# One scaling for both halves of a tile, a gate product on GpSimd, and a new order of the last keys, in a pooled-attention and mixture-of-experts kernel

## The chip, the cores and the metric

The kernel runs on one core of one Trainium2 chip. The metric is device microseconds (us) of one execution. Three timed executions of the kernel before gave 639.33, 640.91 and 641.08 us; the median is 640.91 us. The profile is of a fourth execution, of 639.47 us.

## What is computed

Two parts follow each other: attention with pooled keys and values, and a mixture of experts that sends each token to one expert.

```python
k_p = k.reshape(B, H, Sp, pool, D).mean(axis=3)          # B=8, H=8, S=576, pool=8, Sp=72, D=64
v_p = v.reshape(B, H, Sp, pool, D).mean(axis=3)
scores = scale * np.matmul(q, k_p.transpose(0, 1, 3, 2))
attn = np.exp(scores - np.max(scores, axis=-1, keepdims=True))
attn = attn / (np.sum(attn, axis=-1, keepdims=True) + 1e-09)
x = np.matmul(attn, v_p)                                  # then 4608 tokens x 512
logits = x @ w_gate + modality_bias[modality_id]          # 8 experts
e_idx = np.argmax(logits, axis=1)                         # gate_w is softmax(logits) at e_idx
out[mask] = gate_w[mask, None] * (np.maximum(x[mask] @ w1[e], 0.0) @ w2[e])
```

## The kernel before, in words

**Attention.** The 4608 tokens are 36 tiles of 128. A step (list `steps`, line 455) is two tiles of one batch, or one mixed tile that takes the last 64 tokens of each of two batches; there are 20 steps for 8 batches. The loop at line 895 runs over `n`: in round `n` the scores of step `n+1` are made while step `n-1` is finished. The order of each engine's instructions is the order in which this loop writes them. One round, in the order of the code, for the two tiles `old[0]` and `old[1]` of step `n-1`:

- `t_pe`, `t_act` (lines 551 to 561): TensorE transposes the exponentials of a tile, ACT copies them out of PSUM.
- `s_pe(n, 1)` (line 509): scores of the second four heads; `t4_pe`, `t4_act`: the same as `t_pe` and `t_act` for the last 16 of each pair's 144 keys.
- `a_pe(old[0])` (line 576): TensorE multiplies the transposed weights with the pooled values. A pair of heads has 2 x 72 = 144 keys: 128 of them are one contraction against `vw` (line 590), and the last 16 of all four pairs stand together in one 64-row contraction against `v4` (line 594). The result of a tile lies in two PSUM banks, `av0` for heads 0 to 3 and `av1` for heads 4 to 7, one buffer each. Beside 64 value columns each head has 8 columns of gate logits and one of the sum of weights, 73 (`VC`) in all.
- `s_dve(n, 1)` (line 529): DVE takes the row maximum from the scores (`mx`, line 533) and subtracts it (`sb`, line 536).
- `x_dve(old[0])` (line 596): DVE divides. For each bank it scales the sum (`r`, line 610), inverts it (line 612), writes the 256 values of four heads (`xb`, line 614) and their 32 logits (`lg`, line 616).
- `s_act(n, 1)` (line 540): ACT takes the exponentials of the first 128 keys of each pair (line 548) and of the last 16 (line 549), which go to a region of their own in `pe`.
- `s_pe(n+1, 0)`, `q_pe(n+2, 0)` (transposes of the queries, line 501), `s_dve(n+1, 0)`, then `a_pe(old[1])` and `x_dve(old[1])`.

Between these, `gap(m)` (line 469) lets up to m waiting DVE operations of the routing go (list `drip`): sorting of tokens to experts, written by `route` (line 646) and let go from round 6 on.

**Pooling and value operands.** Keys and values are pooled by GpSimd in three halving additions (`fold`, lines 296 to 298), in the order `pool_v(b+1)`, then `pool_k(b+2)`, one batch after the other; only batch 0 and part of batch 1 go to DVE. `v_operand(b)` (line 356) writes the pooled values into `vw` and `v4`, masked so that each key meets only its own head (line 361: GpSimd's masked product for `v4`), and transposes them (lines 366, 367). `v_gate(b)` (line 374) multiplies the transposed values with the gate matrix (lines 382, 383) and writes the eight gate columns: ACT writes those of `vw` (lines 385, 386), DVE those of `v4` (line 387), as a product with the mask `m_4`. For b over 0 the matmuls of `v_gate` write a free corner of the score bank `sc_1` (line 378), so that bank's next scores (lines 520, 526) wait until lines 385 to 387 have read it.

**Loads.** SP issues the loads in the order of `step_loads` (line 856), one queue, and each load waits until the eighth load before it has landed. `load_v4(b)` (line 220) brings the 16 last pooled rows of each head pair to 64 partitions, twice (`z`), 128 KB each; `load_q(b)` (line 227) brings 1 MB of queries.

**Mixture of experts.** From line 976 on, slots of 256 tokens go through two layers (lines 162 and 1143) in split fp32r precision; DVE and ACT split the weights (lines 135, 138). No line of this part is changed.

Of the kernel before, what the change touches and what calls it, by code (L numbers as in the profile page):

```python
# [9 lines left out]
F32 = mybir.dt.float32  # L10
# [5 lines left out]
ALU = mybir.AluOpType  # L16
# [6 lines left out]
P = 128  # L23
# [7 lines left out]
def kernel(  # L31
# [151 lines left out]
    with ExitStack() as actx:  # L183
        ap = actx.enter_context(tc.tile_pool(name="ap", bufs=1))

        late_p = actx.enter_context(tc.tile_pool(name="late_p", bufs=1))
        ps_av = actx.enter_context(tc.tile_pool(name="ps_av", bufs=1, space=PSUM))
# [4 lines left out]
        def rows_of(x, b):  # L192

            return x[b].rearrange("h (s u) d -> (h s) (u d)", u=POOL)
# [24 lines left out]

        def load_v4(b):  # L220
            t4 = ap.tile([P, POOL * HD], F32, tag="v4", bufs=2, name=f"v4_{b}")
            src = rows_of(v, b).rearrange("(c r) x -> r c x", r=2 * SPL)[P:]
            for z in range(2):
                nc.sync.dma_start(t4[64 * z:64 * z + 64], src)
            v4raw[b] = t4
# [37 lines left out]
        nc.scalar.activation(m_4[:, 0:1], m_a, AF.Exp)  # L263

        m_i = ap.tile([P, NPAIR], I32, name="m_i")
        nc.gpsimd.iota(m_i, pattern=[[-1, NPAIR]], base=P, channel_multiplier=1)
        nc.vector.tensor_single_scalar(m_i, m_i, NPAIR - 1, op=ALU.bitwise_and)
        nc.vector.tensor_single_scalar(m_4, m_i, 0.0, op=ALU.is_equal)
        for z in range(2):
            nc.gpsimd.memset(pt4z[z][64 - 64 * z:128 - 64 * z], 0.0)  # L270
# [83 lines left out]
        m4b = m_4.rearrange("p (j o) -> p j o", o=1)  # L354
# [19 lines left out]
        def v_gate(b):  # L374
            vt, vt4 = vts[b]
            dw, d4 = vw[b % NB], v4[b % NB]
            if b:
                pg = spare[1][:, 1, 4 * SPL:4 * SPL + 12 * E].rearrange("p (u x) -> p u x", u=3)
            else:
                pg = ps_tr.tile([P, 3, 4 * E], F32, tag="tr", name=f"pg_{b}")  # L380
            for u in range(2):
                nc.tensor.matmul(pg[:, u, :], vt[:, u, :], wgb[:, u].rearrange("p g x -> p (g x)"), start=True, stop=True)
            nc.tensor.matmul(pg[:, 2, :], vt4, wg[0:64, 1::2, :], start=True, stop=True)
            pgv = pg[:, 0:2, :].rearrange("p u (g a e) -> p (u g) a e", g=2, a=2)
            nc.scalar.activation(dw[:, :, 0, HD:HD + E], pgv[:, :, 0, :], AF.Copy, scale=m_a)
            nc.scalar.activation(dw[:, :, 1, HD:HD + E], pgv[:, :, 1, :], AF.Copy, scale=m_b)
            nc.vector.tensor_tensor(d4[:, :, HD:HD + E], pg[:, 2, :].rearrange("p (j e) -> p j e", j=NPAIR),
                                    m4b.to_broadcast([P, NPAIR, E]), op=ALU.mult)


        bias_all = ap.tile([P, NT, E], F32, name="bias_all")
# [89 lines left out]
        qts, pqs, scs, pes, pps, pts, avs, lgs = {}, {}, {}, {}, {}, {}, {}, {}  # L481
# [94 lines left out]
        def a_pe(t):  # L576
            n, z = tile_step[t]
            b, jj, _ = steps[n]
            pt, pt4 = pts.pop(t), pt4z[z]
            av = [ps_av.tile([P, 512], F32, tag=f"av{u}", name=f"av_{t}_{u}") for u in range(2)]  # L580
            avs[t] = av
            if jj is not None:
                halves = [(slice(0, P), b % NB)]
            else:
                halves = [(slice(64 * y, 64 * y + 64), (b - 1 + y) % NB) for y in range(2)]
            for u in range(2):
                for gg in range(2):
                    c = 2 * u + gg
                    for hs, y in halves:
                        nc.tensor.matmul(av[u][hs, 2 * VC * gg:2 * VC * (gg + 1)], pt[:, c, hs],  # L590
                                         vw[y][:, c].rearrange("p a x -> p (a x)"), start=(gg == 0), stop=False)
                dst4 = av[u][:, 0:4 * VC].rearrange("p (g x) -> p g x", g=2)[:, :, VC:2 * VC]
                for hs, y in halves:
                    nc.tensor.matmul(dst4[hs], pt4[:, hs], v4[y][:, 2 * u:2 * u + 2, :], start=False, stop=True)  # L594

        def x_dve(t):
            n, z = tile_step[t]
            g, gi = tile_group[t]
            av = avs.pop(t)
            mixed = steps[n][1] is None  # L600
            b = steps[n][0]
            if gi == 0:
                lgs[g] = late_p.tile([P, GT, H, E], F32, tag="lg", bufs=2, name=f"lg_{g}")
            xw = xbs[n if n < NX0 else NX0 + n % (len(xbs) - NX0)]
            xo = xw[:, z, 0:D]
            for u in range(2):
                avv = av[u][:, 0:4 * VC].rearrange("p (h x) -> p h x", h=4)
                r = ap.tile([P, 4], F32, tag="r", bufs=4, name=f"r_{t}_{u}")
                rb = r.rearrange("p (h o) -> p h o", o=1)
                nc.vector.tensor_scalar(r, avv[:, :, VC - 1], float(POOL), 1e-9 * POOL, op0=ALU.mult, op1=ALU.add)  # L610
                gap(1)
                nc.vector.reciprocal(r, r)
                gap(1)
                nc.vector.tensor_tensor(xo[:, u * D // 2:(u + 1) * D // 2].rearrange("p (h d) -> p h d", h=4), avv[:, :, 0:HD],  # L614
                                        rb.to_broadcast([P, 4, HD]), op=ALU.mult)
                nc.vector.tensor_tensor(lgs[g][:, gi, 4 * u:4 * u + 4, :], avv[:, :, HD:HD + E],  # L616
                                        rb.to_broadcast([P, 4, E]), op=ALU.mult)

            if mixed:
                for y in range(2):  # L620
                    r0 = (b - 1 + y) * S + 512
                    stores.append(lambda y=y, r0=r0: nc.sync.dma_start(xs[r0:r0 + 64, :], xw[64 * y:64 * y + 64, 0, :]))
            elif z == 1:
                jj = steps[n][1]
                stores.append(lambda: nc.sync.dma_start(
                    xs[b * S:b * S + 512, :].rearrange("(p j) x -> p j x", j=4)[:, 2 * jj:2 * jj + 2, :], xw))
# [173 lines left out]
        for n, (b, jj, _) in enumerate(steps):  # L800
            if b + 1 < B:
                if jj == 0:
                    m = n if b else n + 1
                    at(hook_0, m, lambda b=b: pool_v(b + 1))
                    at(hook_1, m, lambda b=b: k_operand(b + 1, 0))
                    at(hook_1 if b == 0 else hook_q if b % 2 else hook_3, m, lambda b=b: k_operand(b + 1, 1))
                if jj == 1:
                    m = n if b else n + 1
                    if b + 2 < B:
                        at(hook_0, m, lambda b=b: pool_k(b + 2))  # L810
                    at(hook_1, m, lambda b=b: v_operand(b + 1))
                    at(hook_2, m, lambda b=b: v_gate(b + 1))
# [67 lines left out]
        pool_v(0)  # L880
        gate_operand()
        s_act(0, 0)
        q_pe(1, 0)
        q_act(1, 0)
# [10 lines left out]
        for n in range(N + 1):  # L895
# [45 lines left out]
            if has:  # L941
                s_act(n, 1)
# [18 lines left out]
            if n == 0:  # L961
                v_gate(0)
# [18 lines left out]
    op = [[ps_op.tile([P, 512], F32, name=f"op{i}_{z}") for z in range(2)] for i in range(2)]  # L981
# [119 lines left out]
    t = table(c4 + 6, NCOL, 4)  # L1101
# [189 lines left out]
```

## Time and profile before

| what | value |
|---|---|
| three timed executions, median | 640.91 us |
| profiled execution, its own time | 639.47 us |
| profiled span, first to last instruction | 637.8 us |
| TensorE (PE) busy | 601.1 us, 94% |
| VectorE (DVE) busy | 433.8 us, 68% |
| ScalarE (ACT) busy | 343.8 us, 54% |
| GpSimd (POOL) busy | 198.9 us, 31% |
| first and last `a_pe` matmul (line 590) starts | 24.7 and 190.6 us |
| `xb` products (line 614) | 72, mean 422 ns |

Between the span and the execution's own time lie 1.67 us. The attention's last round ends near 192 us, and the rest is the mixture of experts, in which PE is busy without a pause. The shares of the whole span are averages over both parts; what the change touches lies in the first 192 us.

### The profile page before, as it was taken

The numbers are of one execution on the slowest core, as the hardware profiler recorded it, in microseconds if no ns is written. First come the engines' busy times: TensorE is split into PE (matmuls) and PEld (weight loads), VectorE is DVE, ScalarE is ACT, GpSimd is POOL, SyncE is SP. The second block draws the span as 40 slices with busy tenths as digits, with TensorE's granted clock in tenths as the row PEclk, the third lists the DMA queues.
The fourth block names the chain that finished last, engine by engine and source line by source line (L and its number), as shares of the span: only waits on it lengthen the run. The fifth ranks groups of instructions, "written<-read, shape, count | busy, mean of one in ns | idle before, by whom it ended". The sixth has DMA issues, their size and how long they took to land.

```text
span 637.8 us, 12547 instructions
## 1 busy us (share of the span) xinstructions
PE 601.1 (94%) x4223; PEld 544.8 (85%) x4223; DVE 433.8 (68%) x940; ACT 343.8 (54%) x640; POOL 198.9 (31%) x277
## 2 busy tenths in 40 slices
PE   4799898989899999999999999999999999999992
PEld 3699797888798999999999999999999999999881
DVE  4778989999977578666566566656656566656541
ACT  2667566677441455555555555555556555555530
POOL 6689967563000221320320221231131231131230
PEclk9899999999999999999999999999999999999997
DMA  9999979764201901201210461220225410120120
GB/s 255 290 300 337 350 208 362 223 202 143 67 35 51 315 33 36 68 34 35 68 41 28 148 201 51 67 65 8 63 75 180 145 55 17 52 68 18 51 75 17
DMA packets 63406, 77.18 MB, mean 121 GB/s; under 512 B 15455, under 2 KB 42079, under 8 KB 63328
## 3 DMA queue, kind: packets, MB, share of 16 engines
q1 hardware_dynamic: 57168, 55.98, 28.4%
q0 software_dynamic: 6160, 20.26, 9.7%
q8 instruction: 38, 0.62, 0.4%
q14 instruction: 40, 0.33, 0.2%
HBM read 119.94 MB, written 19.45 MB: 219 GB/s over the span
## 4 chain that ended last, share of the span: by engine, by line
PE 76%; DVE 13%; DMA 7%; issue 1%; ACT 1%; SPq 0%; DVEq 0%; ACTq 0%
PE op L1143 30%; PE hp L162 30%; DMA out_dram<-ob,sidx 6%; PE av L590 3%; PE sc L526 3%; PE xt L153 2%; DVE mx L533 2%; DVE sb L536 2%; PE av L594 2%; DVE xb L614 2%; PE pq L501 1%; PE ph L162 1%; PE pp L555 1%; DVE arow L717 1%; DMA k<-in_k_dram 1%
## 5 line engine op out<-in xcount | busy, mean ns | idle before, releaser
L135 ACT CAST hl<-raw 128x1024 fp32r<-128x1024 f32 x138 | 144.8, 1049 | 138.6 <-PE op L1143 136.6
L162 PE MATMUL hp<-xh,hl 128*128 128x256 f32 x1152 | 186.2, 284 | 0.6 <-issue 0.6
L162 PEld LDWEIGHTS hp<-xh,hl 128*128 128x128 f32 x1152 | 166.0, 189 | 11.5 <-issue 1.0
L138 DVE TENSOR_TENSOR hl<-raw,hl 128x1024 fp32r<-128x1024 f32 x144 | 174.8, 1215 | 0.0
L1143 PE MATMUL op<-hl,hh 128*128 128x512 f32 x554 | 173.5, 394 | 0.0
L1129 POOL DMA_INDIRECT out_dram<-ob,sidx x37 | 51.0, 1379 | 369.3 <-DVE ob L1125 260.2
L166 DVE SCALAR_TENSOR_TENSOR hlo<-hp,hh 128x256 fp32r<-128x256 f32 x139 | 58.8, 423 | 136.6 <-ACT hh L164 136.6
L1143 PE MATMUL op<-hl,hlo 128*128 128x512 f32 x277 | 108.4, 391 | 0.0
L1143 PEld LDWEIGHTS op<-hl,hh 128*128 128x128 f32 x554 | 94.8, 189 | 12.1
L162 PE MATMUL hp<-xl,hl 128*128 128x256 f32 x576 | 92.0, 282 | 0.0
L164 ACT ACTIVATE hh<-hp 128x256 fp32r<-128x256 f32 x139 | 53.4, 384 | 49.6 <-PE hp L162 49.6
L162 PEld LDWEIGHTS hp<-xl,hl 128*128 128x128 f32 x576 | 79.0, 190 | 0.0
L1143 PEld LDWEIGHTS op<-hl,hlo 128*128 128x128 f32 x277 | 52.0, 188 | 11.8
L590 PE MATMUL av<-vw,pt 128*128 128x146 f32 (+1 forms) x320 | 50.9, 299 | 4.9 <-DVE lg L616 3.7
L142 POOL DMA_INDIRECT xg<-xs,gidx x40 | 44.2, 1105 | 17.1 <-issue 8.9
L590 PEld LDWEIGHTS av<-vw,pt 128*128 128x128 f32 (+1 forms) x320 | 40.3, 183 | 7.9 <-DVE lg L616 4.9
L526 PE MATMUL sc<-kt,qt 128*128 128x144 f32 x256 | 38.3, 294 | 1.5 <-DVE rs L706 1.1
L526 PEld LDWEIGHTS sc<-kt,qt 128*128 128x128 f32 x256 | 34.1, 195 | 2.4 <-DVE rs L706 1.3
L156 DVE TENSOR_TENSOR xl<-xt,xh 128x512 fp32r<-128x512 f32 x38 | 24.5, 684 | 15.5 <-ACT xh L155 15.5
L560 ACT COPY pt<-pp 128x512 f32<-128x512 f32 x36 | 21.1, 586 | 25.4 <-PE pp L555 25.0
L533 DVE TENSOR_REDUCE mx<-sc 128x8 f32<-128x576 f32 (+1 forms) x40 | 27.7, 692 | 10.0 <-PE sc L526 7.6
L614 DVE TENSOR_TENSOR xb<-av,r 128x256 f32<-128x256 f32 x72 | 30.4, 422 | 1.6
(226 smaller groups left out, 710.5 us busy)
## 6 DMA issues: line engine op xcount, KB each, us to landing
raw<-in_moe_w_dram SPq DMA_DIRECT2D x304, 256.0 KB
xs<-xb SPq DMA_DIRECT2D x16, 528.0 KB
k<-in_k_dram SPq DMA_DIRECT2D x7, 1024.0 KB
v<-in_v_dram SPq DMA_DIRECT2D x7, 1024.0 KB
q<-in_q_dram SPq DMA_DIRECT2D x6, 1024.0 KB
q<-in_q_dram SPq DMA_DIRECT2D x4, 512.0 KB
v<-in_v_dram SPq DMA_DIRECT2D x16, 128.0 KB
xs<-xb SPq DMA_DIRECT2D x8, 132.0 KB
```

Source lines behind the costliest of these rows:

```text
L135: nc.scalar.copy(hl[f][:, 0, :], raw[f])
L138: eng.tensor_sub(hl[f][:, 1, :], raw[f], hl[f][:, 0, :].bitcast(F32))
L142: nc.gpsimd.indirect_dma_start(out=xgs[(2 * s + tt) % len(xgs)], out_offset=None, in_=xs[0:rows, :], in_offset=IndirectOffsetOnAxis(idx[:, ...
L162: nc.tensor.matmul(ph, hl[f][:, w, d * P:(d + 1) * P], x[:, d, :], start=(n == 0 and d == 0), stop=(n == 2 and d == ND - 1))
L164: nc.scalar.activation(hh, ph, AF.Relu)
L166: nc.vector.scalar_tensor_tensor(hlo, ph, 0.0, hh.bitcast(F32), op0=ALU.max, op1=ALU.subtract)
L526: nc.tensor.matmul(dst, qt[:, i, :], kt[b % NB][:, :, h * SPL:(h + 1) * SPL], start=True, stop=True)
L533: nc.vector.reduce_max(mx, scv, axis=AX.X)
L590: nc.tensor.matmul(av[u][hs, 2 * VC * gg:2 * VC * (gg + 1)], pt[:, c, hs], vw[y][:, c].rearrange("p a x -> p (a x)"), start=(gg == 0), sto ...
L614: nc.vector.tensor_tensor(xo[:, u * D // 2:(u + 1) * D // 2].rearrange("p (h d) -> p h d", h=4), avv[:, :, 0:HD], rb.to_broadcast([P, 4, H ...
L1129: nc.gpsimd.indirect_dma_start(out=out[:, :], out_offset=IndirectOffsetOnAxis(idx.bitcast(U32), 0), in_=ob, in_offset=None, bounds_check=N ...
L1143: nc.tensor.matmul(o[tt], l[:, ts_], hl[f][:, w, D:2 * D], start=(f == 0 and n == 0), stop=(f == NF - 1 and n == 2))
```

## The change

Four things change.

1. The two PSUM banks of a tile become one tile `av` of two banks. `x_dve` scales the sums of all eight heads in one operation, inverts them in one, writes all 64 logits in one, and then writes the values bank by bank. The logits now stand ahead of the values. Two of the four `gap(1)` calls go, and a `gap(2)` follows the tile.
2. The gate product of `v4`: ACT copies the 32 columns out of PSUM into a new SBUF tile `vg4`, and GpSimd multiplies them with the mask. DVE no longer takes part.
3. The last keys' exponentials are written in another order: the 16 weights of a head pair stand side by side, where before the four pairs alternated.
4. With that order the mask `m_4` and the load of `v4` change: row 16 c + s of the tile holds row s of pair c, where before it was row 4 s + c. The source's access pattern in DRAM was 16 rows x 4 pairs x 512 values and is now 4 pairs x 16 rows x 512 values, with the same 64 partitions as destination.

```diff
-            src = rows_of(v, b).rearrange("(c r) x -> r c x", r=2 * SPL)[P:]
+            src = rows_of(v, b).rearrange("(c r) x -> c r x", r=2 * SPL)[:, P:, :]
...
-        nc.gpsimd.iota(m_i, pattern=[[-1, NPAIR]], base=P, channel_multiplier=1)
-        nc.vector.tensor_single_scalar(m_i, m_i, NPAIR - 1, op=ALU.bitwise_and)
+        nc.gpsimd.iota(m_i, pattern=[[-16, NPAIR]], base=P, channel_multiplier=1)
+        nc.vector.tensor_single_scalar(m_i, m_i, 16 * (NPAIR - 1), op=ALU.bitwise_and)
...
-            nc.vector.tensor_tensor(d4[:, :, HD:HD + E], pg[:, 2, :].rearrange("p (j e) -> p j e", j=NPAIR),
-                                    m4b.to_broadcast([P, NPAIR, E]), op=ALU.mult)
+            vg4 = ap.tile([P, NPAIR, E], F32, tag="vg4", bufs=1, name=f"vg4_{b}")
+            nc.scalar.copy(vg4, pg[:, 2, :].rearrange("p (j e) -> p j e", j=NPAIR))
+            nc.gpsimd.tensor_tensor(d4[:, :, HD:HD + E], vg4, m4b.to_broadcast([P, NPAIR, E]), op=ALU.mult)
...
-            tail = pe[:, 2 * NPAIR * P:].rearrange("p (t s c) -> p t c s", t=2, c=NPAIR)[:, 0:nt, 2 * w:2 * w + 2, :]
+            tail = pe[:, 2 * NPAIR * P:].rearrange("p (t c s) -> p t c s", t=2, c=NPAIR)[:, 0:nt, 2 * w:2 * w + 2, :]
...
-            av = [ps_av.tile([P, 512], F32, tag=f"av{u}", name=f"av_{t}_{u}") for u in range(2)]
+            av = ps_av.tile([P, 2, 512], F32, tag="av", name=f"av_{t}")
...
+            avv = av[:, :, 0:4 * VC].rearrange("p u (h x) -> p u h x", h=4)
+            r = ap.tile([P, 2, 4], F32, tag="r", bufs=4, name=f"r_{t}")
+            rb = r.rearrange("p u (h o) -> p u h o", o=1)
+            nc.vector.tensor_scalar(r, avv[:, :, :, VC - 1], float(POOL), 1e-9 * POOL, op0=ALU.mult, op1=ALU.add)
+            gap(1)
+            nc.vector.reciprocal(r, r)
+            gap(1)
+            nc.vector.tensor_tensor(lgs[g][:, gi].rearrange("p (u h) e -> p u h e", u=2), avv[:, :, :, HD:HD + E],
+                                    rb.to_broadcast([P, 2, 4, E]), op=ALU.mult)
             for u in range(2):
...
+                nc.vector.tensor_tensor(xo[:, u * D // 2:(u + 1) * D // 2].rearrange("p (h d) -> p h d", h=4),
+                                        avv[:, u, :, 0:HD], rb[:, u].to_broadcast([P, 4, HD]), op=ALU.mult)
+            gap(2)
```

DVE in round 6, where the first routing operations are let go, for the first tile of step 5 (`r`, `xb`, `lg` belong to the tile; `lgr`, `m`, `oh` and `sm` to the routing). Before:

```order
L610 TENSOR_SCALAR r_0_1056<-av_0_1030 128x4
L666 TENSOR_REDUCE m_0_989<-lgr_987 128x9
L612 RECIPROCAL r_0_1056<-r_0_1056 128x4
L669 TENSOR_TENSOR lgr_987<-lgr_987,m_0_989 128x72
L614 TENSOR_TENSOR xb_172<-av_0_1030,r_0_1056 128x256
L616 TENSOR_TENSOR lg_1055<-av_0_1030,r_0_1056 128x32
L610 TENSOR_SCALAR r_1_1064<-av_1_1031 128x4
L673 SCALAR_TENSOR_TENSOR lgr_987<-lgr_987,w_166 128x72
L612 RECIPROCAL r_1_1064<-r_1_1064 128x4
L674 TENSOR_REDUCE m_0_990<-lgr_987 128x9
L614 TENSOR_TENSOR xb_172<-av_1_1031,r_1_1064 128x256
L616 TENSOR_TENSOR lg_1055<-av_1_1031,r_1_1064 128x32
```

The same tile with the change (line numbers are those of the changed file):

```order
L610 TENSOR_SCALAR r_1016<-av_991 128x8
L668 TENSOR_REDUCE m_0_950<-lgr_948 128x9
L612 RECIPROCAL r_1016<-r_1016 128x8
L671 TENSOR_TENSOR lgr_948<-lgr_948,m_0_950 128x72
L614 TENSOR_TENSOR lg_1015<-av_991,r_1016 128x64
L617 TENSOR_TENSOR xb_172<-av_991,r_1016 128x256 x2
L675 SCALAR_TENSOR_TENSOR lgr_948<-lgr_948,w_166 128x72
L676 TENSOR_REDUCE m_0_951<-lgr_948 128x9
```

Eight operations of the tile became five, and two of the four routing operations that stood inside the tile moved behind it. The first operation now reads both banks; the first matmul of the next tile waits for the last one.

GpSimd in rounds 4 and 5, between the product of `v4` for batch 2 (line 361) and the pooling of the values of batch 3. Before:

```order
L298 TENSOR_TENSOR kp_3_717<-k_3_353 64x64
L361 TENSOR_TENSOR vw_139<-vp_2_616,m_143 128x4x64
L296 TENSOR_TENSOR v_351<-v_351 128x2x256
L297 TENSOR_TENSOR v_351<-v_351 128x2x128
L298 TENSOR_TENSOR vp_842<-v_351 128x128
```

With the change:

```order
L298 TENSOR_TENSOR kp_3_696<-k_3_355 64x64
L361 TENSOR_TENSOR vw_139<-vp_2_600,m_143 128x4x64
L389 TENSOR_TENSOR vw_139<-vg_2_792,m_143 128x4x8
L296 TENSOR_TENSOR v_353<-v_353 128x2x256
L297 TENSOR_TENSOR v_353<-v_353 128x2x128
L298 TENSOR_TENSOR vp_813<-v_353 128x128
```

The gate product of a batch (line 389) stands behind line 361 of the same batch and ahead of the pooling of the next batch's values, and it waits for ACT's copy.

More of the change, by code (lines that the diff above doesn't have):

```diff
@@ L589, in a_pe @@
                     for hs, y in halves:
-                        nc.tensor.matmul(av[u][hs, 2 * VC * gg:2 * VC * (gg + 1)], pt[:, c, hs],
+                        nc.tensor.matmul(av[hs, u, 2 * VC * gg:2 * VC * (gg + 1)], pt[:, c, hs],
                                          vw[y][:, c].rearrange("p a x -> p (a x)"), start=(gg == 0), stop=False)
-                dst4 = av[u][:, 0:4 * VC].rearrange("p (g x) -> p g x", g=2)[:, :, VC:2 * VC]
+                dst4 = av[:, u, 0:4 * VC].rearrange("p (g x) -> p g x", g=2)[:, :, VC:2 * VC]
                 for hs, y in halves:
@@ L605, in x_dve @@
             xo = xw[:, z, 0:D]
-            for u in range(2):
[L607 to L617, printed above, removed]
+            avv = av[:, :, 0:4 * VC].rearrange("p u (h x) -> p u h x", h=4)
[7 more added lines that the diff above has]
+                                    rb.to_broadcast([P, 2, 4, E]), op=ALU.mult)
+            for u in range(2):
+                nc.vector.tensor_tensor(xo[:, u * D // 2:(u + 1) * D // 2].rearrange("p (h d) -> p h d", h=4),
+                                        avv[:, u, :, 0:HD], rb[:, u].to_broadcast([P, 4, HD]), op=ALU.mult)
+            gap(2)
             if mixed:
```

## The prediction

> **What bounds the kernel now.** I read the stages first: busy time of each engine in stretches of 20 us (columns: PE, its weight loads, DVE, ACT, POOL, each with its instruction count, then clock, DMA share, GB/s).
>
> ```profile
> 20.00:40.00 20.00, 18.03 (x130) 16.01 (x131) 14.40 (x42) 11.95 (x34) 15.24 (x26) 0.91 1.07 314
> 40.00:60.00 20.00, 19.97 (x173) 18.71 (x172) 15.96 (x54) 14.77 (x38) 18.59 (x30) 1.00 1.04 302
> 60.00:80.00 20.00, 16.99 (x133) 14.72 (x132) 19.42 (x63) 11.01 (x32) 18.50 (x29) 1.00 1.06 357
> 80.00:100.00 20.00, 19.70 (x174) 18.02 (x173) 18.34 (x66) 13.66 (x35) 13.66 (x22) 1.00 0.79 237
> 100.00:120.00 20.00, 17.48 (x141) 15.52 (x140) 19.29 (x65) 12.25 (x34) 13.69 (x23) 1.00 0.85 278
> 120.00:140.00 20.00, 18.28 (x161) 16.48 (x160) 19.30 (x58) 15.20 (x37) 11.68 (x20) 1.00 0.73 234
> 140.00:160.00 20.00, 18.83 (x172) 17.50 (x171) 19.37 (x73) 16.05 (x42) 4.86 (x5) 1.00 0.49 162
> 160.00:180.00 20.00, 16.82 (x151) 15.48 (x150) 19.37 (x68) 9.06 (x22) 0.00 (x0) 1.00 0.16 43
> 180.00:200.00 20.00, 20.00 (x148) 18.45 (x147) 13.57 (x60) 5.45 (x14) 0.00 (x0) 1.00 0.15 56
> ```
>
> The reader is to see three regimes. Up to 80 us the DMA engines are full (1.04 to 1.07). From 60 to 180 us DVE is the fullest engine: 115.1 of 120 us, while PE has 108.1. From 180 us on PE has no pause. So DVE time that goes is worth at most the 11.9 us that PE lacks between 60 and 180 us, of which 3.0 lie before 80 us and 8.9 behind. The view of the waits, for PE from 60 to 200 us (total, times, longest), names DVE for nearly all of it, these two first:
>
> ```profile
> PE av L590 <- DVE lg L616: 3.7, 4, 1.3
> PE sc L520 <- DVE vw L387: 3.5, 3, 1.3
> ```
>
> The first is the hand-over of a tile's PSUM banks, the second the gate product in the score bank. Both are edited.
>
> **Fewer DVE operations.** The timeline of DVE, one tile without routing between its operations (start, duration):
>
> ```profile
> 104.08 0.15 DVE L610 TENSOR_SCALAR r<-av 128x4 f32<-128x4 f32 x1
> 104.27 0.18 DVE L612 RECIPROCAL r<-r 128x4 f32<-128x4 f32 x1
> 104.48 0.42 DVE L614 TENSOR_TENSOR xb<-av,r 128x256 f32<-128x256 f32 x1
> 104.82 0.18 DVE L616 TENSOR_TENSOR lg<-av,r 128x32 f32<-128x32 f32 x1
> 104.92 0.15 DVE L610 TENSOR_SCALAR r<-av 128x4 f32<-128x4 f32 x1
> ```
>
> From start to start the four operations take 0.19, 0.21, 0.34 and 0.10 us, 0.84 for a bank and 1.68 for both. With the change: 0.19 + 0.21 + 0.13 (64 logits, an estimate: the 0.10 of 32 and a little) + 2 x 0.34 = 1.21, so some 0.46 us less per tile, and 0.1 us per batch for line 387. For the 25 tiles whose DVE work falls between 60 and 180 us that is 11.5 us.
>
> It doesn't all reach PE, because the hand-over gets coarser. Before, bank 0 was free 0.84 us into the tile's DVE work and bank 1 at 1.68. The two banks' contractions (four matmuls of line 590 and two of line 594) start some 0.8 us apart, as the rows at 70 us below show by their 0.77 for the first four, so a waiting PE could go at about 0.9. Now it goes at 1.21 plus whatever routing stands inside, and DVE can't begin until both banks are done. So a stall with n tiles of DVE backlog behind it shrinks by about 0.46 n - 0.3. Between 80 and 140 us PE lacks only 0.3 us in the first stretch and about 2 in each of the next two, so PE leads again and again, DVE catches up between the stalls, and n is 1 or 2: I take 0.8 us for all of it. From 140 to 180 us DVE has 38.7 of 40 us and never catches up: 8 tiles, of which 7 lie ahead of the last stall, 0.46 x 7 - 0.3 = 2.9; PE lacks 4.35 there; I take 2.5. Bounds: nothing, and the whole 8.9 us.
>
> **The gate product.** ACT's copy is priced by its neighbour of the same 32 columns (line 386), GpSimd's product from above by line 361, which has eight times the elements. The timeline around batch 4:
>
> ```profile
> 90.58 0.61 POOL L361 TENSOR_TENSOR vw<-vp,m 128x256 f32<-128x256 f32 x1
> ...
> 93.93 0.28 ACT L386 ACTIVATE vw<-sc,m_b 128x32 f32<-128x32 f32 x1
> ...
> 95.87 0.17 DVE L387 TENSOR_TENSOR vw<-sc,m 128x32 f32<-128x32 f32 x1
> ...
> 103.96 0.46 POOL L298 TENSOR_TENSOR kp<-k 128x128 f32<-128x128 f32 x1 [3.90 <-PE pk L332]
> ```
>
> The score bank is free at about 94.5 instead of 96.04, since the copy doesn't queue behind DVE's `sb`; that removes the waits named `vw`. The price is on GpSimd: the product stands ahead of the next values' pooling, which followed line 361 at 91.2, and now waits until 94.5, 3.3 us later. Behind it come those values and then the next keys, whose last addition waited 3.90 us for PE: it was ready at 100.06, will be at 103.4, and still isn't late at 103.96. I cost it at nothing; without that cover it is 3.3 us a batch, and up to 0.6 us more for the product.
>
> **Last keys in runs of 16.** ACT has 9 to 16 of every 20 us behind 80 us, and no wait of PE above 0.2 us there is for it. Eight more copies of 0.28 are 2.2 us on ACT; shorter exponentials of line 549 may give some of it back. Nothing of this lies on the path, by the same cover: ACT's idle time.
>
> **The load of the last values.** Its source was 16 outer blocks of 4 rows and is 4 outer blocks of 16 rows. A transfer has to be cut up among the 16 DMA engines. No transfer of this trace has fewer than 16 outer blocks, so the price is bounded from both sides: as before, or all of it on 4 engines. I take the second, which is the cut along the outer blocks. From the page for 0 to 80 us (DMA queues, then issues):
>
> ```profile
> q1 hardware_dynamic: 21506, 24.46, 103.3%
> ...
> v<-in_v_dram SPq DMA_DIRECT2D x12, 128.0 KB
> ```
>
> At the 357 GB/s of 60 to 80 us one of 16 engines moves 22.3 KB per us. A load of 131 KB puts 8.2 KB on each of 16 engines (0.37 us) or 32.8 KB on each of four (1.47 us): 1.10 us more, 2.2 us per batch, since each batch is loaded twice. By the mean of the 80 us (24.46 MB) it is 2.6. With the engines full, four of them fall behind by that much per batch, and every load behind needs all sixteen.
>
> The Trainium skill's page "DMA: Bandwidth & Descriptors" (section "Why a DMA increments its semaphore by 16 and not by 1") states that a transfer takes the largest number of engines, up to 16, that divides the slowest dimension of both access patterns; here that would be 16 before and 4 after. By it the sum is the one below, without it that of the first rival. No run so far shows it.
>
> What waits for a load, from SP's waits and from the timeline:
>
> ```profile
> SPq L625 <- DMA q<-in_q_dram: 3.1, 1, 3.1
> ```
>
> ```profile
> 33.16 1.28 POOL L296 TENSOR_TENSOR k<-k 128x512 f32<-128x512 f32 x1 [1.28 <-DMA k<-in_k_dram]
> ...
> 48.04 0.27 PE L367 MATMUL pv<-ident,vp 128*64 128x128 f32 x1
> ...
> 67.20 0.34 SPq L625 DMA_DIRECT2D xs<-xb  x1
> ...
> 68.17 0.66 PE L501 MATMUL pq<-ident,q 128*128 128x128 f32 x4
> ...
> 70.22 0.77 PE L590 MATMUL av<-vw,pt 128*128 128x146 f32 x4 [0.41 <-DVE lg L616]
> ...
> 73.88 0.71 PE L520 MATMUL sc<-kt,qt 128*64 128x144 f32 x8 [1.31 <-DVE vw L387]
> ```
>
> GpSimd waited for the keys of batch 2 at 33.16 us; with these and then the values of batch 2 it was busy nearly throughout until PE took them at 48.04. Two batches' last values are loaded ahead of those keys: 4.4 us, which come through to PE. The queries of batch 3 landed just before 67.20 us (the store issued there had waited 3.1 us for them), and PE used them at 68.17: 1.0 us to spare. Four batches' last values are loaded ahead of them: 8.8 - 1.0 = **7.8 us later** (9.3 by the other price); the earlier delay is inside this one. Behind 80 us the DMA share is 0.85 and less, so nothing is added there.
>
> While PE stands at that point DVE catches up, and PE's next two waits, at 70.22 and 73.88, go: -1.7.
>
> **Sum.** +7.8 - 1.7 - 0.8 - 2.5 = +2.8 us. On the profiled execution's 639.47 (span 637.8 and 1.67 around it) that is 642.3. This execution lies 1.44 us under the median of the three timed ones, 640.91, which is the better base for runs to come: **643.7 us**.
>
> **Rivals.**
> 1. The transfer is spread as before. Then only the DVE side is left: 0.6 of the 3.0 us that PE lacks from 60 to 80 us (two tiles behind: 0.46 x 2 - 0.3), 0.8 and 2.5, so -3.9, **637.0 us**, and down to 632 if the coarser hand-over costs less than I think. For it: nothing here shows a transfer on four engines. Against it: 16 blocks became 4. Chance 0.25.
> 2. Slow loads, but DVE's saving counts in full behind 80 us: 16 tiles x 0.46 = 7.4, under PE's 8.9. Then 7.8 - 1.7 - 7.4 = -1.3, **639.6**. For it: DVE at 97%. Against it: the coarser hand-over. Chance 0.10.
> 3. Slow loads, and the coarse hand-over becomes a stall of its own at line 590 where PE leads. PE has some 2 us of other work from one tile's contraction to the next; the hand-over takes 1.2 plus two routing operations, so it decides where these take over 0.8 us together. At 0.4 us for some 14 tiles it adds 5.6: **649**. For it: line 590's waits are already the largest. Against it: most routing operations take 0.2. Chance 0.05.
>
> That the change saves nothing on DVE is no rival: the operations are gone from its order.
>
> **How the numbers follow.** The forecast has 0.60; its own range is 639.5 to 648. The range of all cases, 634.5 to 648.5, leaves out the far end of rival 1 and rival 3. About 0.3% (1.9 us) is what a measurement of this kernel can tell from no change. Forecast: slower 0.41, same 0.16, faster 0.03; rival 1: faster 0.24, same 0.01; rival 2: faster 0.03, same 0.06, slower 0.01; rival 3: slower 0.05. Together slower 0.47, same 0.23, faster 0.30.
>
> **What would show it.** Right: waits of PE or GpSimd for a DMA between 34 and 80 us that weren't there, the transposes of batch 3's queries about 8 us later, and a shorter distance from there to the last contraction. The tile's five DVE operations at 1.2 us; waits of line 590 for the second `xb` instead of `lg`, none of the scores for the gate product. GpSimd waiting up to 4 us for ACT ahead of the values' pooling, with its later waits for PE shorter by as much. Wrong: no wait for a DMA behind 34 us (rival 1), or PE's lack behind 80 us gone (rival 2), or line 590's waits grown (rival 3).

## The result, and the profile after

Five executions of the changed kernel took 644.08 to 645.19 us, median **644.33**; five of the kernel before 639.33 to 641.56, median 641.08. The ratio is 1.0053, 95% interval 1.0036 to 1.0069: slower by 3.25 us, where +2.8 was forecast. The profiled span is 642.4 us, 4.6 more than before: the two profiled executions (644.08 and 639.47 us) lie further apart than the medians, since the one of the kernel before is nearly its fastest.

The stages of the changed kernel (columns as in the prediction):

```profile
20.00:40.00 20.00, 14.61 (x104) 12.51 (x105) 10.86 (x23) 9.74 (x29) 11.12 (x21) 0.91 0.93 245
40.00:60.00 20.00, 18.35 (x159) 17.09 (x157) 12.05 (x30) 13.90 (x38) 18.43 (x33) 1.00 0.90 250
60.00:180.00 120.00, 110.52 (x941) 101.21 (x941) 103.18 (x311) 78.33 (x213) 69.88 (x112) 0.99 0.77 242
```

Two things stand against each other. From 20 to 60 us the DMA engines, full before (1.07 and 1.04), are at 0.93 and 0.90 and move 245 and 250 GB/s instead of 314 and 302, and PE loses 3.4 and 1.6 us of work. From 60 to 180 us DVE is busy 103.2 us instead of 115.1, and PE 110.5 instead of 108.1.

How far PE is behind the kernel before can be read at any instruction, since both kernels run the same matmuls. First the kernel before, then the changed one, at transposes of queries (in brackets PE's idle time and what ended it):

```profile
45.60 0.60 PE L501 MATMUL pq<-ident,q 128*128 128x128 f32 x4
...
77.17 0.60 PE L501 MATMUL pq<-ident,q 128*128 128x128 f32 x4
...
125.12 0.66 PE L501 MATMUL pq<-ident,q 128*128 128x128 f32 x4
...
127.07 0.60 PE L501 MATMUL pq<-ident,q 128*128 128x128 f32 x4
...
168.36 0.66 PE L501 MATMUL pq<-ident,q 128*128 128x128 f32 x4
```

```profile
34.06 0.63 PE L502 MATMUL pq<-ident,q 128*128 128x128 f32 x4 [3.18 <-DMA q<-in_q_dram]
...
52.84 0.63 PE L502 MATMUL pq<-ident,q 128*128 128x128 f32 x4 [1.64 <-DMA q<-in_q_dram]
...
77.70 0.63 PE L502 MATMUL pq<-ident,q 128*128 128x128 f32 x4 [1.51 <-ACT pe L550]
...
85.45 0.60 PE L502 MATMUL pq<-ident,q 128*128 128x128 f32 x4
...
131.25 0.66 PE L502 MATMUL pq<-ident,q 128*128 128x128 f32 x4
...
135.19 0.66 PE L502 MATMUL pq<-ident,q 128*128 128x128 f32 x4 [1.83 <-ACT kt L339]
...
173.40 0.66 PE L502 MATMUL pq<-ident,q 128*128 128x128 f32 x4
```

| place | before | after | behind |
|---|---|---|---|
| queries of batch 2 | 45.60 | 52.84 | +7.2 |
| queries of batch 3 | 68.17 | 77.70 | +9.5 |
| next but one step | 77.17 | 85.45 | +8.3 |
| ahead of the stall at 135 us | 125.12 | 131.25 | +6.1 |
| behind it | 127.07 | 135.19 | +8.1 |
| last queries | 168.36 | 173.40 | +5.0 |
| end of span | 637.8 | 642.4 | +4.6 |

At 77.70 the profile names an ACT instruction, though ACT had copied the last queries' bank out by 76.9. SP had a store at 77.63 that waited 1.2 us for the same queries' load, as the store at 67.20 waited 3.1 before; I read the wait at 77.70 as one for that load.

DVE's tile and GpSimd's product, both as written in the signs of the prediction:

```profile
109.40 0.15 DVE L610 TENSOR_SCALAR r<-av 128x8 f32<-128x8 f32 x1
109.58 0.20 DVE L612 RECIPROCAL r<-r 128x8 f32<-128x8 f32 x1
109.82 0.22 DVE L614 TENSOR_TENSOR lg<-av,r 128x64 f32<-128x64 f32 x1
109.96 0.75 DVE L617 TENSOR_TENSOR xb<-av,r 128x256 f32<-128x256 f32 x2
110.62 0.75 DVE L534 TENSOR_REDUCE mx<-sc 128x8 f32<-128x576 f32 x1
```

```profile
POOL vw L389 <- ACT vg L388: 12.5, 4, 5.9
```

From 109.40 to the next operation at 110.62 are 1.22 us (1.21 in the prediction). GpSimd waits for ACT 12.5 us in four places, 5.9 at most, where "up to 4" was expected. PE's largest wait at the contraction is now the one for the second `xb` (60 to 200 us), and none of its waits there is for the gate product:

```profile
PE av L591 <- DVE xb L617: 2.5, 2, 1.6
```

### The profile page after: what moved, and what is told of

Same layout as the page of the kernel before. It is cut to its first block, busy times and chain, and to the rows that moved or that the text cites. A ratio compares the mean times of both kernels' runs of the same rounds, so it can differ in the third digit from the quotient of the medians.

```text
span 642.4 us, 12423 instructions
## 1 busy us (share of the span) xinstructions
PE 602.2 (94%) x4223; PEld 546.6 (85%) x4223; DVE 416.6 (65%) x824; ACT 343.2 (53%) x648; POOL 201.9 (31%) x285
## 2 busy tenths in 40 slices
DMA packets 63213, 77.17 MB, mean 120 GB/s; under 512 B 15263, under 2 KB 41887, under 8 KB 63136
## 4 chain that ended last, share of the span: by engine, by line
PE 69%; DMA 13%; DVE 7%; SPq 4%; issue 4%; ACT 1%; POOL 1%; POOLq 0%; DVEq 0%; ACTq 0%
PE op L1145 28%; PE hp L162 27%; DMA out_dram<-ob,sidx 7%; PE av L591 3%; DMA q<-in_q_dram 3%; PE xt L153 2%; PE sc L527 2%; DMA v<-in_v_dram 2%; PE ph L162 1%; PE av L595 1%; DMA k<-in_k_dram 1%; DVE hl L138 1%; PE pp L556 1%; PE pq L502 1%; DVE mx L534 1%
## 5 line engine op out<-in xcount | busy, mean ns | idle before, releaser
L135 ACT CAST hl<-raw 128x1024 fp32r<-128x1024 f32 x138 | 144.8, 1049 | 138.6 <-PE op L1145 135.6
L1131 POOL DMA_INDIRECT out_dram<-ob,sidx x37 | 52.3, 1413 | 366.6 <-DVE ob L1127 262.1
L591 PE MATMUL av<-vw,pt 128*128 128x146 f32 (+1 forms) x320 | 50.5, 297 | 3.2 <-DVE xb L617 2.5
L595 PE MATMUL av<-vw,pt 128*128 128x146 f32 (+1 forms) x160 | 30.7, 295 | 0.0
```

Source lines behind the costliest of these rows:

```text
L135: nc.scalar.copy(hl[f][:, 0, :], raw[f])
L591: nc.tensor.matmul(av[hs, u, 2 * VC * gg:2 * VC * (gg + 1)], pt[:, c, hs], vw[y][:, c].rearrange("p a x -> p (a x)"), start=(gg == 0), sto ...
L1131: nc.gpsimd.indirect_dma_start(out=out[:, :], out_offset=IndirectOffsetOnAxis(idx.bitcast(U32), 0), in_=ob, in_offset=None, bounds_check=N ...
```

## The experiments

Theory L says that the load of the last values runs on few DMA engines and makes all later loads late. Rival G says that the time is lost on GpSimd, by its wait for ACT. The three parts are called M (merge on DVE), G (gate product), R (last keys with their load). All differences below are to the kernel before on the same chip, whose median was 640.3 to 641.1. The last column is read from the one profiled execution of each kernel; e3's is the fastest of its twelve (634.72 us) and e8's the slowest of its six (651.13), so in these two rows the profile is not that of a typical execution.

| kernel | parts | us | ratio, 95% interval | to before | last queries |
|---|---|---|---|---|---|
| before | - | 641.08 | | | 168.36 |
| changed | M G R | 644.33 | 1.0036 to 1.0069 | +3.3 | 173.40 |
| e1 | M G | 632.56 | 0.9858 to 0.9889 | -8.2 | 161.39 |
| e11, e1 again | M G | 632.67 | 0.9852 to 0.9898 | -7.7 | 161.31 |
| e2 | R | 648.89 | 1.0108 to 1.0138 | +8.2 | 177.44 |
| e3 | M | 639.32 | 0.9957 to 0.9993 | -1.2 | 164.68 |
| e4 | G | 634.89 | 0.9897 to 0.9936 | -5.7 | 162.50 |
| e7 | M R | 646.79 | 1.0065 to 1.0117 | +6.5 | 177.77 |
| e8 | G R | 649.30 | 1.0101 to 1.0150 | +9.0 | 178.17 |
| e6_hand | coarse hand-over alone | 646.89 | 1.0079 to 1.0132 | +6.3 | 173.56 |
| e10 | G and half of M | 634.30 | 0.9880 to 0.9932 | -6.0 | 163.06 |
| e5 | M G R, load in 8 | 651.00 | 1.0128 to 1.0183 | +10.3 | 180.09 |
| e6_two | M G R, load in 4 | 660.57 | 1.0283 to 1.0319 | +19.9 | 189.96 |
| e9 | M G, R without its load | 641.22 | 0.9993 to 1.0019 | +0.7 | 163.23 |

**The last keys undone (e1), and once more (e11).**

```diff
-            src = rows_of(v, b).rearrange("(c r) x -> c r x", r=2 * SPL)[:, P:, :]
+            src = rows_of(v, b).rearrange("(c r) x -> r c x", r=2 * SPL)[P:]
...
-            tail = pe[:, 2 * NPAIR * P:].rearrange("p (t c s) -> p t c s", t=2, c=NPAIR)[:, 0:nt, 2 * w:2 * w + 2, :]
+            tail = pe[:, 2 * NPAIR * P:].rearrange("p (t s c) -> p t c s", t=2, c=NPAIR)[:, 0:nt, 2 * w:2 * w + 2, :]
```

(and the mask's two lines as before)

> The changed kernel with the last keys as before (load in 16 outer blocks of 4 rows, mask and tail of the weights as before); DVE's merged operations and the gate product on ACT and GpSimd stay. Theory L (the load of the last values is confined to a few DMA engines, and every load behind it is late): the queries of batch 3 are used at about 68 us again instead of 77.7, the waits of PE for queries at 34.06 and 52.84 go, and the time is that of the first rival of the prediction, 637 us, between 634 and 639. Rival G (the time is lost on GpSimd, which waits 12.5 us for ACT ahead of the gate product and starts its pooling later): 643 to 645, with the same waits of GpSimd for ACT.

> The changed kernel with the last keys as before, a second time, on the same chip as the half merge: 632 to 633.5 as the first time.

632.56 and 632.67 us: faster than the 634 to 639 that L expected, and 11.4 us under the changed kernel by the differences to before. In e1, with GpSimd still waiting 8.5 us for ACT, the batch 3 queries are taken 0.7 us later than before (68.17), and the next ones at 75.42:

```profile
68.83 0.66 PE L502 MATMUL pq<-ident,q 128*128 128x128 f32 x4
...
75.42 0.60 PE L502 MATMUL pq<-ident,q 128*128 128x128 f32 x4
...
161.39 0.66 PE L502 MATMUL pq<-ident,q 128*128 128x128 f32 x4
```

**The last keys alone (e2).** The diff is the opposite, on the kernel before.

> The kernel before with only the last keys changed (load in 4 outer blocks of 16 rows, mask and tail in runs of 16). Theory L: the queries of batch 3 are used about 9.5 us later; 1.7 us of that are swallowed by waits that follow, and up to 2 come on top where a later expert's weights are late: 647 to 651 us. Rival G: this has no work for GpSimd added, so 640 to 642.

648.89 us. Rival G falls: no work of GpSimd was added here. From 0 to 80 us PE waits for queries 8.5 us in four places in this kernel, and 1.1 us in one place in the kernel before:

```profile
PE pq L501 <- DMA q<-in_q_dram: 8.5, 4, 3.2
```

**The load's order alone (e9).** The changed kernel with only the first line of e1's diff.

> The changed kernel with only the order of the load's blocks as before (16 outer blocks of 4 rows), its mask and the tail of the weights still in runs of 16, so the last values stand in other rows than the weights mean: the sums over the last keys are other ones, the work is the same. Theory L (all the loss is in the load): 632 to 633.5, as the kernel with the last keys undone. If the tail's copies in runs of 16 gain or lose something of their own, the difference to 632.6 is it. If the loss is not in the load: 643 to 645.

641.22 us, but the whole time says little. The other rows under the same weights change the logits, so that tokens go to other experts: this kernel has 18 matmuls more (4241 instructions on PE, in the first line of its page, instead of 4223), and the stretch from its last queries to the end of the span is 476.7 us instead of 469.0.

```profile
PE 606.4 (95%) x4241; PEld 550.6 (86%) x4241; DVE 416.0 (65%) x824; ACT 343.6 (54%) x649; POOL 202.3 (32%) x286
```

The attention part has the same work as before, and there the last queries come at 163.23, against 173.40 in the changed kernel and 161.39 in e1. The order of the load's blocks is thus 10.2 of the 12.0 us between these two in the profiled executions. The other 1.8 arise in e9 between the queries at 59.76 and at 77.27 us (59.63 and 75.42 in e1), where e9 has a stretch at half clock (last section); behind it the two run in step, so the mask and the copies in runs of 16 cost nothing that can be seen.

The 12.0 us themselves lie in three places, and in between the changed kernel and e1 run in step: 8.9 up to the queries of batch 3 (77.70, in e1 68.83), 1.2 in the step behind them, which the changed kernel runs in part at half clock (85.45, in e1 75.42), and 2.0 at the stall at 135.19 us (in e1 123.14), to which the third term of the account below comes back.

**How many engines.** The page's line of packets, for the kernel before, the changed one, e5 (each load in four, one per block of 16 rows) and e6_two (each load in two, of two blocks):

```profile
DMA packets 63406, 77.18 MB, mean 121 GB/s; under 512 B 15455, under 2 KB 42079, under 8 KB 63328
```

```profile
DMA packets 63213, 77.17 MB, mean 120 GB/s; under 512 B 15263, under 2 KB 41887, under 8 KB 63136
```

```profile
DMA packets 64175, 77.19 MB, mean 119 GB/s; under 512 B 16224, under 2 KB 42848, under 8 KB 64097
```

```profile
DMA packets 63214, 77.18 MB, mean 117 GB/s; under 512 B 15263, under 2 KB 41887, under 8 KB 63136
```

The rows of values are 2 KB each and there are as many as before, so it is the small packets that count. If each engine that takes part ends its share with one small packet, 16 loads on 16 engines have 256 and on four have 64: 192 fewer, and the line shows 15455 - 15263 = 192. Then e5's 64 loads on 16 engines each make 1024, 768 more than before (769 are there), and e6_two's 32 loads on two make 64, as in the changed kernel (the same 15263). The Trainium skill's page "DMA: Bandwidth & Descriptors" (section "Why a DMA increments its semaphore by 16 and not by 1") has the rule that the slowest dimension sets the number of engines: by it 16, 4, 16 and 2, and the traces agree.

```diff
-                nc.sync.dma_start(t4[64 * z:64 * z + 64], src)
+                for c in range(0, NPAIR, 2):
+                    nc.sync.dma_start(t4[64 * z + 16 * c:64 * z + 16 * c + 32], src[c:c + 2])
```

> The changed kernel with each load of last values cut into two, of two outer blocks of 16 rows. If a transfer takes as many engines as its slowest dimension allows and always begins with the same ones, two engines carry all of it, 2.9 us more per batch than in the changed kernel; four batches lie ahead of the queries of batch 3, so these come 8 to 12 us later still and the time is 651 to 657 us. If each half takes another pair: 643 to 646, as the changed kernel. If the number of outer blocks doesn't matter: as it, too, but then the cut into single blocks gains nothing either.

660.57 us, 3.6 above the top of the range that was expected if the same two engines carry it all. The queries of batch 3 come at 84.08 us, only 6.4 later than in the changed kernel, where 8 to 12 were expected; the rest is lost behind them, in waits for queries up to 129.63. PE waits for queries in six places:

```profile
  DMA q<-in_q_dram: 16.4, 6
```

```diff
-                nc.sync.dma_start(t4[64 * z:64 * z + 64], src)
+                for c in range(NPAIR):
+                    nc.sync.dma_start(t4[64 * z + 16 * c:64 * z + 16 * c + 16], src[c])
```

> The changed kernel with its layout of the last keys, each load cut into four, one for each block of 16 rows (16 outer blocks of one row each, 32 KB), so eight loads per batch instead of two. Theory L: spread over 16 engines again, so the queries of batch 3 are at 68 to 70 us and the time is that of the kernel with the last keys undone, 634 to 641 with the price of six more issues per batch. If the loss is in the layout itself (mask, copies in runs of 16, weights): 643 to 646.

651.00 us: the expectation of L failed, though the load is on 16 engines, and PE takes the queries of batch 3 at 79.96 us, later still than the changed kernel. Two views of e5, the stages and SP's waits from 0 to 100 us, show another bound:

```profile
0.00:20.00 20.00, 10.75 (x53) 8.83 (x53) 11.33 (x17) 7.54 (x18) 11.41 (x52) 1.00 0.76 206
20.00:40.00 20.00, 15.57 (x111) 13.54 (x111) 11.05 (x26) 10.80 (x33) 10.46 (x17) 0.91 0.92 269
40.00:60.00 20.00, 15.80 (x122) 14.53 (x120) 9.78 (x23) 10.11 (x29) 18.43 (x33) 0.91 0.81 250
60.00:80.00 20.00, 16.00 (x130) 14.68 (x129) 17.75 (x51) 12.28 (x35) 16.17 (x27) 1.00 0.83 246
```

```profile
SPq L225 <- DMA v<-in_v_dram: 8.1, 4, 2.8
SPq L225 <- DMA q<-in_q_dram: 8.0, 4, 3.5
SPq L225 <- DMA k<-in_k_dram: 7.0, 7, 3.7
```

Each load waits until the eighth before it has landed. Eight loads of 32 KB fill that queue, and SP stands at them for 23.1 us until loads of queries, keys and values ahead have landed, so the engines are at 0.76 to 0.92. I took the price of six more issues as small; I read the loss as the price of the queue's length. That this is all of it was not separated.

**The merge alone (e3), and its hand-over alone (e6_hand).** e3 is part M of the change on the kernel before, with the new tile of the first diff here and the operations of the second; e6_hand has the first alone and keeps all four DVE operations for each bank:

```diff
-            av = [ps_av.tile([P, 512], F32, tag=f"av{u}", name=f"av_{t}_{u}") for u in range(2)]
+            av = ps_av.tile([P, 2, 512], F32, tag="av", name=f"av_{t}")
...
-                avv = av[u][:, 0:4 * VC].rearrange("p (h x) -> p h x", h=4)
+                avv = av[:, u, 0:4 * VC].rearrange("p (h x) -> p h x", h=4)
```

```diff
-                nc.vector.reciprocal(r, r)
+            nc.vector.tensor_scalar(r, avv[:, :, :, VC - 1], float(POOL), 1e-9 * POOL, op0=ALU.mult, op1=ALU.add)
+            gap(1)
+            nc.vector.reciprocal(r, r)
...
```

> The kernel before with only the merge: one PSUM tile of two banks, scaling, reciprocal and logits once for both banks. Gate product and last keys as before. The merge and the gate product together gave -8.2 us (632.6 against 640.7). Theory D (DVE's 0.46 us a tile is what PE waits for): -3 to -6, 635 to 638. Theory G (most of the gain is the score bank, which no longer waits for DVE's gate product): 0 to -3, 638 to 641.

> The kernel before with only the hand-over made coarse: one PSUM tile of two banks, but all four DVE operations still once for each bank. The prediction priced the coarse hand-over at 0.3 us for each stall of PE, and at 0.4 us for 14 tiles in its third rival: +1.5 to +5.6, 642 to 646, with longer waits of PE at the contraction's first line. If the hand-over costs nothing: 640 to 641.5.

e3: 639.32 us, e6_hand: 646.89, 0.9 above its range. The coarse hand-over alone costs 6.3 us, and the rest of part M gives 7.6 back (639.3 against 646.9): the fewer operations, with two of the routing's operations moved out of the tile. PE's waits at the contraction, from 0 to 200 us, in e6_hand and in e3:

```profile
PE av L590 <- DVE lg L616: 9.3, 12, 1.8
```

```profile
PE av L590 <- DVE xb L616: 3.3, 4, 1.4
```

Twelve waits where the kernel before has four (3.7 us, from 0 to 200 as well as from 60 to 200), then four again, these in the fastest of e3's executions. By the medians, the merge is two large terms with opposite signs.

**The gate product alone (e4).** Part G on the kernel before:

```diff
-            nc.vector.tensor_tensor(d4[:, :, HD:HD + E], pg[:, 2, :].rearrange("p (j e) -> p j e", j=NPAIR),
-                                    m4b.to_broadcast([P, NPAIR, E]), op=ALU.mult)
+            nc.scalar.copy(vg4, pg[:, 2, :].rearrange("p (j e) -> p j e", j=NPAIR))
+            nc.gpsimd.tensor_tensor(d4[:, :, HD:HD + E], vg4, m4b.to_broadcast([P, NPAIR, E]), op=ALU.mult)
```

> The kernel before with only the gate product by way of ACT's copy and GpSimd. Theory D: PE's waits for that product go (3.9 us in the trace of before), but DVE, at 97% between 100 and 180 us, takes most of that back at the next hand-over, since only 0.2 us a batch leave it: 0 to -2.5, 638 to 641. Theory G: -4 to -6, 635 to 637. If GpSimd's wait for ACT costs something: above 641.

634.89 us: the second theory of these two expectations (the score bank) has it. DVE does not take the gain back at the next hand-over; the waits there get shorter as well, 1.2 and 1.0 us from 0 to 200:

```profile
PE av L591 <- DVE lg L617: 1.2, 3, 0.4
...
PE av L591 <- DVE r L611: 1.0, 2, 0.8
```

**One part undone (e7, e8).** e7 is the changed kernel with e4's diff taken back, so with line 387 of before; e8 is the changed kernel with both of e3's diffs taken back, so with two tiles and the loop over the banks.

> The changed kernel with the gate product back on DVE: merge and new last keys. Theory A (the parts add up as they measured alone: merge -1.2, gate product -5.7, last keys +8.2): 647.5 us. Theory B (while PE waits for loads DVE catches up, so what DVE or the score bank would have cost is partly hidden): 644.5 to 646.5, since the gate product's waits are then partly hidden.

> The changed kernel with scaling, reciprocal and logits once for each bank again: gate product and new last keys. Theory A: 640.6 - 5.7 + 8.2 = 643.1 us, so a little faster than the changed kernel at 644.3. Theory B: 645 to 648, with PE's waits at the contraction's first line for the logits back.

646.79 and 649.30 us. e7 fits the sum of single parts within a us (-1.2 + 8.2 = +7.0, measured +6.5); e8 is 6.5 above that sum (-5.7 + 8.2 = +2.5, measured +9.0), and above theory B's range too. So the parts don't add up where G meets R without M: the gate product gives 5.7 us alone, and nothing beside R alone (648.9 and 649.3). In e8 GpSimd's wait for ACT has grown:

```profile
POOL vw L389 <- ACT vg L388: 16.0, 5, 7.7
```

But this wait does not reach PE where e8 loses most. At the queries at 124.22 us e8 is 10.5 us behind e4 (113.73), and at 140.99 us 15.5 (125.49); e2 loses only 1.1 on the kernel before in the same piece. In it PE waits for nothing of GpSimd's. It waits 1.0 us for DVE and 2.6 for a copy of keys on ACT, and runs at half clock from 138.6 us on:

```profile
137.45 0.66 PE L502 MATMUL pq<-ident,q 128*128 128x128 f32 x4 [2.57 <-ACT kt L339]
```

Why G brings these about beside R, no run isolates; e8's profiled execution is also its slowest.

**Half the merge (e10).** On e4, with the two banks still two tiles:

```diff
+            r = ap.tile([P, 2, 4], F32, tag="r", bufs=4, name=f"r_{t}")
             for u in range(2):
-                nc.vector.tensor_scalar(r, avv[:, :, VC - 1], float(POOL), 1e-9 * POOL, op0=ALU.mult, op1=ALU.add)
+                nc.vector.tensor_scalar(r[:, u], avv[u][:, :, VC - 1], float(POOL), 1e-9 * POOL, op0=ALU.mult, op1=ALU.add)
+            gap(1)
+            nc.vector.reciprocal(r, r)
...
```

> The kernel before with the gate product by way of ACT and GpSimd, and the merge by half: the sums are scaled bank by bank, inverted once, values and logits bank by bank; the two banks stay two tiles, so that bank 0 is free after about 1.0 us and bank 1 after 1.45 (0.19 + 0.19 + 0.21 + 2 x 0.44), DVE 0.2 us a tile more than with the whole merge. If the fine hand-over is worth more than 0.2 us of DVE: 630 to 632, under the changed kernel with its last keys undone (632.6). If DVE's total decides: 633 to 635, between that and the gate product alone (634.9).

634.30 us: the time is the one that the second case there gave, in which DVE's total decides; e11, the same kernel as e1, at 632.67 on the same chip stays the fastest. The version that beats both kernels is thus the change without its part R, at 0.9875 of the kernel before.

## Why the prediction was right, point by point

The forecast was +2.8 us, and +3.25 was measured. Its mechanism stood: the load on four engines makes the later loads late, and DVE's saving pays part of it back. That the sum came so near is in part luck. The 1.7 us of swallowed waits are part of the price of the late loads, so the forecast for R alone is 7.8 - 1.7 = +6.1, where e2 measured +8.2; what is left for M and G beside it is -0.8 - 2.5 = -3.3, where -4.9 was measured (3.3 - 8.2). The two misses, 2.1 and 1.6 us, nearly cancel. The terms, by the table of the first section (profiled executions, together +4.6):

1. **Four engines.** Right, by the small packets, e9 and e6_two. The queries of batch 3 came +9.5 us late, not +7.8; the price from the mean over 80 us gave 9.3. As in the prediction, part of it is not the load's: without R (e1) PE takes them 0.7 us later than before, so the load makes 8.9.
2. **The next waits are swallowed, -1.7.** PE was +9.5 behind at 77.70 and +8.3 at 85.45: -1.25, near the forecast by luck. For this step the kernel before needs 9.00 us, the changed one 7.75, and e1, where no load is late, 6.59: M and G take these waits away by themselves, and the changed kernel loses 1.2 us in it at half clock. In e2, which has neither M nor G, the step takes 7.80, also in part at half clock; there the late load does it.
3. **-0.8 from 80 to 140 us.** From +8.3 to +6.1 at 131 us, so -2.1, and then a stall that was not in the sum, +2.0. Of it the prediction said that behind 80 us "nothing is added". ACT stood for the load of an expert's weights, and the copy of the keys, `kt`, stands behind that cast in ACT's order (the profile names a store as what ended the wait; the cast reads `raw`, whose load SP issued at 127.00 us, so I read it as a wait for that load):

```profile
133.99 0.62 ACT L818 CAST hl<-raw 128x512 fp32r<-128x512 f32 x1 [3.32 <-DMA xs<-gate]
134.51 0.31 ACT L338 COPY kt<-pk 64x192 f32<-64x192 f32 x1
```

The keys were transposed at 131.94. e2 (1.2 us), e5 (1.4), e8 (2.6) and e6_two (3.5) have the same wait, the kernel before, e1 and e9 don't; e7, whose loads are late too, hasn't it either in its profiled execution. That step failed: free DMA engines don't make a late load harmless, because the queue that issues the loads is late too. SP issued the first of these weights at 116.59 us, before at 101.86.

4. **-2.5 from 140 to 180 us.** From +8.1 to +5.0: -3.1.
5. **The gate product at nothing on GpSimd, its gain in the waits named `vw`.** Right for e4 and e1, where 8.8 and 8.5 us of GpSimd's waiting lie beside other work. But the sum has no term for the gain beyond the wait at 73.88, and the gate product alone gives 5.7. Beside late loads and M it gives 3.2 (e7 to the changed kernel); where the rest goes is open.
6. **The rivals.** Rival 1's mechanism, the spread load, was tried as e1: 632.6, not 637.0. Its -3.9 was half of the measured -8.2: it is a price for DVE's fewer operations, and these give 1.2 alone (e3), while the gate product, taken as a small part since DVE was to be the bound either way, gives 5.7 alone (e4). Rival 2 did not come: PE still lacked 9.5 us from 60 to 180. Rival 3's mechanism is real: the coarse hand-over costs 6.3 us by itself, near the 5.6 it was priced at, and not the 0.3 us per stall of the forecast; but the other half of the merge pays for it with 7.6.

## What to carry to other kernels

A load with few outer blocks ran on as few DMA engines here: where the engines are full, look at the slowest dimension of the source pattern before changing a layout, and count the small packets afterwards. Cutting such a load into more transfers did not mend it in e5, where the queue holds a fixed number of them. A merge of operations across two buffers has two prices, the operations that go and the hand-over that gets coarser; price each alone, since here both (6.3 and 7.6 us) were five to six times the net of 1.2.

## What the runs showed of the hardware

PE's clock falls to half for stretches of 3.4 us (or twice and three times that, 6.8 in e7 and 10.2 in e8), at different places in each kernel. The granted clock (third column from the right) in neighbouring stretches, first of the kernel before, then of the changed one:

```profile
14.79:18.20 3.41, 1.63 (x14) 1.39 (x13) 3.38 (x5) 1.71 (x5) 2.32 (x7) 1.00 1.05 301
18.20:21.62 3.42, 3.22 (x28) 3.07 (x27) 3.12 (x6) 2.97 (x10) 1.79 (x4) 1.00 1.18 190
21.62:25.03 3.41, 2.09 (x13) 1.25 (x12) 3.38 (x6) 1.81 (x7) 1.16 (x3) 0.96 1.07 323
25.03:28.44 3.41, 3.41 (x17) 3.40 (x17) 1.89 (x8) 0.99 (x3) 3.20 (x4) 0.54 1.15 297
```

```profile
31.95:35.36 3.41, 1.30 (x10) 1.33 (x11) 0.00 (x1) 0.58 (x1) 2.94 (x6) 0.97 0.76 224
35.36:38.77 3.41, 3.41 (x19) 2.89 (x18) 1.26 (x5) 0.82 (x4) 0.00 (x0) 0.53 1.04 331
76.32:79.73 3.41, 2.03 (x15) 1.98 (x16) 3.03 (x12) 2.33 (x8) 1.31 (x4) 0.97 1.00 266
79.73:83.14 3.41, 3.41 (x21) 3.07 (x19) 1.34 (x7) 0.43 (x1) 3.25 (x5) 0.53 0.96 322
```

Ahead of these three half-clock stretches PE had been busy for only 1.3 to 2.1 of 3.4 us. Up to 200 us the profiled executions show one such stretch in the kernel before, two in the changed one and in e9, none in e1, e4 and e10, three in e2 and four in e8, of which the first is the one of 10.2 us. The start of the kernel is not counted: there PE is at half speed too, though the clock column has 1.00 (in the kernel before eight matmuls of line 526 take 2.13 us at 12.04 and 1.15 at 14.69).

What a stretch costs is read against e1, which has none. In the step from 77.70 to 85.45 us the changed kernel loses 1.2 us by it, and in e9 the rows from 66.49 to 70.16 take 3.67 us where e1 needs 2.00 (65.87 to 67.87): 1.7, the half of 3.4 that a dense PE would lose. So a pause of PE can cost more than its length. But such a loss can go again at a later wait: behind its stretch the kernel before is 1.45 us behind e1 (28.37 and 26.92), and at 50.24 us 0.1 (50.17 in e1), since e1 has meanwhile waited 1.1 us for pooled values. So none of the 8.2 us that e1 gains comes from this stretch.

The Trainium skill's page "TensorE: Matmul & The Clock Gate" (section "What's actually happening") states half clock after at least one idle window of about 3.4 us. Here the length agrees, but the longest single wait ahead of these three was 3.2 us and PE was busy for part of each window; and a low share alone doesn't do it: the stretch from 14.79 us with 1.63 was not followed by one, nor was e1's from 21.56 to 24.97 with 2.08, at the place where the kernel before has 2.09 and then half clock. What decides is open. In e1:

```profile
21.56:24.97 3.41, 2.08 (x14) 1.25 (x12) 3.41 (x4) 1.81 (x6) 1.58 (x5) 1.00 1.09 297
24.97:28.39 3.42, 2.96 (x24) 2.56 (x26) 2.02 (x7) 2.27 (x7) 3.26 (x4) 1.00 1.14 311
```
